# Another build-time order for the steps of a fused attention and feed-forward kernel

## The chip, the cores and the metric

The kernel runs on one core of a Trainium2 chip. The metric is the device time of one execution in microseconds (us); of several runs the median counts. TensorE (PE) multiplies matrices, with PEld for its weight loads; VectorE (DVE), ScalarE (ACT) and GpSimd (POOL) do elementwise work; SyncE (SP) issues nearly all DMAs. Each engine works through its own queue in order, and an instruction that waits holds up all that stand behind it on that engine.

## The reference

Tokens of width D = 448, S = 2048 of them, in 4 segments of L = 512; 16 heads of 28. The result is x + s * g, where s is a memory-augmented attention and g a gated feed-forward network, both of the normalized input.

```
xn = layernorm(x)
q, k, v = xn @ wq, xn @ wk, xn @ wv            # per head and segment
for each segment:                              # 16 heads
    a_dot = softmax(q k^T * scale + mask) v    # causal within the segment
    a_mem = phi(q) M / (phi(q) z + 1e-6)       # M, z: memory of earlier segments
    o     = sigmoid(beta) * a_mem + (1 - sigmoid(beta)) * a_dot
    M, z += phi(k)^T v, sum(phi(k))            # phi(t) = t + 1 if t > 0 else exp(t)
s = o @ wo
g = silu(gelu(xn @ w_gate) * (xn @ w_up) @ w_down)
out = x + s * g
```

## The kernel before

All work is first written down as steps (`Op`). A step has a name, the engines it may run on with an occupied time and a latency, the steps it depends on (`deps`), steps that must only have begun before it (`after`), buffers that it acquires, and an urgency `prio` (smaller goes first). The function `arrange` then plays the engines' queues forward with these times and picks, engine by engine, the most urgent step among those that can start within 0.2 us of the earliest. The order in which it picks is the order in which the instructions are issued; on the chip the order is fixed and only the waits are real. The times in `arrange` decide nothing but this order.

The stages on TensorE follow each other as G0, A0, A1, G1, A2, G2, A3, G3, D3 (`ORDER`). G*s* is the gate and up projection of segment *s* (`gate_up`), in 14 columns of blocks; A*s* is its attention. Into A*s* other matmuls are mixed: the projections of the next segment, the w_down matmuls of an earlier one and the output projection. To spread them over the ten groups of scores, each such step gets one group in its `after`: the share of the work that is more urgent than the step, times ten, rounded down.

Names of steps, with *s* the segment:

- `bn`, `ag`, `ep`, `pw`, `xn`, `du`, `tr`, `ev`: layernorm of a block of 128 tokens, and its transpose into `xnT` (by TensorE for segment 0, else by a DMA).
- `wq`*sg*, `wk`*sg*, `v`*sb*: projections of q, k, v on TensorE; `evwq`, `evwk`, `evv`: their evictions from PSUM. `pad`: the copy of wq and wk into padded tiles.
- `sc`*sk*: group *k* of scores on TensorE; `ex`*sk0*, `ex`*sk1*: its two exponentials on ScalarE; `mk`: the causal masks on GpSimd; `pv`*sk*: the product with v on TensorE.
- `exwq`, `exwk`, `miwq`, `miwk`, `phwq`, `phwk`: phi of q and k on ScalarE, GpSimd and VectorE; `tk`: the DMA transpose of phi(k) into `pk`; `up`, `macc`, `um`, `ma`, `mc`: the update of the memory.
- `rd`*sg* with two digits: the matmul that reads the memory; `ou`: eviction of an attention or memory result into `oa` or `om`, followed by the store of its denominators to DRAM (`den`).
- Denominators are inverted for all heads at once: `dc` loads them into the tile `dc`, `dg` and `rc` add, scale and invert on VectorE, `rd` with three digits stores the result to `rdr`, `rb` loads it broadcast into the tile `rb`. The last digit of `dc`, `dg` and `rc` is 0 for attention and 1 for memory. Then `sm` multiplies the memory part on GpSimd, `ca` the attention part on VectorE, and `cb` joins them into `oT` on GpSimd.
- `gh`, `gu`: matmuls of gate and up; `ge`: gelu on ScalarE; `hm`: the product into `hT` on VectorE, which frees the PSUM banks for a later `gu`. `dn`*sbk*: five or four w_down matmuls of token block *b*; `th`, `sg`: silu by a tanh; `wo`: output projection; `fm`, `fa`, `st`: product, sum with x, and store.
- `guard`: `sq` (ScalarE) and `rq` (VectorE) sum the squares of wq and wk, `nrm` and `nrm2` reduce them to one flag `oki`. Every engine loads the flag (`load_ok`), and the program branches on it to a slow general version, which does not run here.

The DMA steps are issued by SP in the order that `arrange` gives. Large loads at the start: x, wq, wk, wv, w_gate and w_up first; then, after the transposes of segment 1, x of segments 2 and 3, wo and two halves of w_down (`wd_in0`, `wd_in1`), all of which the w_down matmuls wait for.

Of the kernel before, what the change touches and what calls it, by code (L numbers as in the profile page):

```python
# [14 lines left out]
DRAM = bass.MemoryType.DRAM  # L15
ORDER = mybir.DependencyInfo(mybir.DependencyClass.NoSync, mybir.DependencyReason.DATA)

# [58 lines left out]
        return self.pool.aps[self.slots[i]]  # L76


SEM, SWITCH, TABLE, AHEAD = 0.06, 0.1, 1.29, 0.2
WIDE = ()  # L80
ORDER = {"G0": 0, "A0": 1, "A1": 2, "G1": 3, "A2": 4, "G2": 5, "A3": 6, "G3": 7, "D3": 8}


def arrange(ops):


    free = {e: 0.0 for o in ops for e in o.eng}
    mode, table = "full", "exp"
    blocked, left = {}, {}
    for o in ops:  # L90
        left[o] = len(o.deps) + len(o.after)
        for d in o.deps + o.after:
            blocked.setdefault(d, []).append(o)
    ready = {o: 0.0 for o in ops if not left[o]}
    done, port, lanes, pipe = [], {"DVE": 0.0, "POOL": 0.0}, [], 0.0
    while ready:
        found = []
        for o, t in ready.items():
            picks, taken = [], set()
            for b in o.acq:  # L100
                got = b.pick(taken)
                if got is None:
                    break
                t = max(t, got[0] + SEM)
                taken |= {(got[1], i) for i in got[2]}
                picks.append((b, got[1], got[2]))
            else:
                if o.kb is not None and len(lanes) >= 8:
                    t = max(t, lanes[-8] + SEM)
                for e in o.eng:  # L110
                    u = max(t, free[e])
                    if e == "POOL" or e == "DVE" and o.alone:
                        u = max(u, port["DVE" if e == "POOL" else "POOL"])
                    found.append((u, o.prio, e, o, picks))
        if not found:
            raise RuntimeError("no work can start: " + ", ".join(o.name for o in list(ready)[:20]))
        t0, _, e0, _, _ = min(found, key=lambda c: c[:2])
        s, _, e, o, picks = min((c for c in found if c[2] == e0 and c[0] <= t0 + AHEAD),
                                key=lambda c: c[1])
        occ, lat = o.eng[e]  # L120
        if e == "PE" and o.mode and o.mode != mode:
            s, mode = s + SWITCH, o.mode
        if e == "ACT" and o.act and o.act != table:
            s, table = s + TABLE, o.act
        if e == "POOL" or e == "DVE" and o.alone:
            port[e] = s + occ
        if o.kb is not None:
            pipe = max(s + lat, pipe) + o.kb / o.rate
            lanes.append(pipe)
            lat = pipe - s  # L130
        o.start, o.on, o.done = s, e, s + lat
        free[e] = s + occ
        for b, pool, slots in picks:
            b.take(slots)
        done.append(o)
        del ready[o]
        for n in blocked.get(o, ()):
            left[n] -= 1
            if not left[n]:
                ready[n] = max([0.0] + [d.done + (SEM if d.on not in n.eng else 0.0) for d in n.deps]  # L140
                               + [d.start for d in n.after])
    if len(done) < len(ops):
        raise RuntimeError("work that never gets ready")
    return sorted(done, key=lambda o: o.start)


def fast_path(tc, A_x, A_wq, A_wk, A_wv, A_wo, A_beta, B_w_gate, B_w_up, B_w_down, out):
    nc = tc.nc
    x2 = A_x.flatten_outer_dims()
# [17 lines left out]
    with ExitStack() as ctx:  # L167
# [16 lines left out]
        nhalf = const.tile([P, NB], F32, name="nhalf")  # L184
        warm = const.tile([P, L], BF16, name="warm")
        ones = const.tile([P, 1], F32, name="ones")
# [10 lines left out]
        macc = const.tile([P, G, P], F32, name="macc")  # L197
# [40 lines left out]
        nrm = const.tile([1, 2, H], F32, name="nrm")  # L238
# [4 lines left out]
        ops = []  # L243

        def op(*a, **kw):
            o = Op(*a, **kw)
            ops.append(o)
            return o
# [23 lines left out]
            return op(name, {"POOL": (t, t + 0.05)}, fn, **kw)  # L272

        def dma(name, kb, fn, **kw):
            return op(name, {"SP": (0.55, 2.0)}, fn, kb=kb, **kw)

        def turned(name, fn, **kw):
            return op(name, {"SP": (1.3, 1.5)}, fn, kb=220, **kw)
# [1 line left out]
        def at(phase, n):  # L280
            return 1000.0 * phase + n

        def A(s):
            return ORDER[f"A{s}"]

        def Gp(s):
            return ORDER[f"G{s}"]

# [39 lines left out]
        def fill(eng, name, t, pr, ap, value):  # L328
            return op(name, {eng: (t, t + 0.06)}, lambda: (
                nc.vector if eng == "DVE" else nc.gpsimd).memset(ap, value), prio=pr)  # L330
# [10 lines left out]
        for i, t in enumerate(va_t):  # L341
            va_c.append([fill("POOL", f"va{i}", 0.26, -390 + 300 * i, t[:, :, :, Dh:HP], 0.0)])
            o = va_c[i][0]
# [4 lines left out]
        o = fill("POOL", "bd", 0.4, -80, bdmask[:], 0.0)  # L348
        for i in range(HG):
            o = op(f"bd{i}", {"POOL": (0.15, 0.2)}, lambda i=i: nc.gpsimd.memset(  # L350
                bdmask[i * HP:i * HP + Dh, i * HP:(i + 1) * HP], 1.0), after=[o], prio=-79)
# [41 lines left out]
        def gates():  # L393
# [6 lines left out]
            deps=[g_op], prio=5)  # L400
# [281 lines left out]
        att = {}  # L682

        def attention(s, ph):
            steps = steps_of(0, 1) + steps_of(2, 3)
            sc, exps = [], []
            pts = {}
            acc = {g: Buf(B_, FEW if s in WIDE else ONE) for g in range(G)}
            opened, todo = {}, {g: 4 for g in range(G)}
            late, pvs = {}, []  # L690

            def scores(k):
                S2 = [Buf(B_, THREE if s in WIDE else TWO) for _ in range(2)]
                st = steps[k]
# [240 lines left out]
        def load_ok():  # L935
            got["ok"] = nc.values_load(oki[0:1, 0:1], min_val=0, max_val=1)
# [4 lines left out]
        def where_ahead(s):  # L941
            def f(nm, n):
                if s == LAST and (nm == "wv" or n > 1):
                    return at(A(s), {"wv": 1, "wq": 6, "wk": 7}[nm] + 2 * n)
                return at(A(s - 1), 20 + {"wv": 64 + 8 * n, "wq": 16 * n, "wk": 16 * n + 8}[nm])
            return f
# [5 lines left out]
        ok_op = guard(at(Gp(0), 60))  # L952
        for s in range(NSEG):
            if s < LAST:
                project(s + 1, where_ahead(s + 1), ONE)
            attention(s, A(s))
            for half in range(2):
                if s > 0:
                    phi(s, "wq", half, at(A(s), 20 + 20 * half))
                if s < LAST:  # L960
                    phi(s, "wk", half, at(A(s), 30 + 20 * half))
            if s > 0:
                read(s, at(A(s), 60))
            if s < LAST:
                update(s, at(A(s), 120))
            d = max(s - 1, 0)
            for b in range(NB):
                if s == 1 and b < 3 or s == 0 and b >= 3:
                    continue
                down(d, b, at(A(s), 12 + 24 * (b if s else 2 * b)))  # L970
            if s == 1:
                combine(0, at(A(1), 5))
            if s > 0:
                for b in range(NB):
                    finish(d, b, at(A(s), 90 + 10 * b))
            if s == 0:
                layer_norm(2, at(A(0), 100))
            else:
                gate_up(s, Gp(s))
                tabled.clear()  # L980
                combine(s, at(Gp(s), 40))
            if s == 1:
                layer_norm(3, at(Gp(s), 100))
                op("ok", {"V": (0.0, 0.0)}, load_ok, deps=[ok_op], after=[att["sc_end"]])
        for b in range(NB):
            down(LAST, b, at(8, 10 * b))
            finish(LAST, b, at(8, 10 * b + 15))
# [4 lines left out]
        for s in range(NSEG):  # L992
            work = sorted((o for o in ops if "PE" in o.eng and at(A(s), 0) <= o.prio < at(A(s), 400)),
                          key=lambda o: o.prio)
            total, sofar = sum(o.eng["PE"][0] for o in work), 0.0
            for o in work:
                k = int(sofar / total * len(att[s]))
                sofar += o.eng["PE"][0]
                if k > 0:
                    o.after.append(att[s][k - 1])  # L1000

        with tc.manual_schedule():
            for o in arrange(ops):
                if o.fn is not None:
                    o.fn()
        fast_path.ops = ops
        return got["ok"]

# [381 lines left out]
```

## Time and profile before

| | us |
|---|---|
| median of 3 runs | 249.37 (248.83 to 251.12) |
| profiled execution | 250.88 |
| its span, from the first to the last instruction | 249.0 |
| TensorE busy | 233.2 |
| VectorE, ScalarE, GpSimd busy | 161.4, 151.4, 133.5 |
| mean granted TensorE clock | 0.986 |

The times of all shown rows are microseconds from the start of the span, from one profiled execution. In a timeline row stand the start, the length, the engine, the source line, the operation with its output and inputs, and in brackets how long the engine was idle before and what ended that. The letter q behind an engine's name means its sequencer: for SP the issue of a DMA. Busy times of TensorE include the tails of matmuls that overlap the next.

### The profile page before, as it was taken

Reading aid. Unit: us, or ns where it says so; the run is one execution under the profiler, and the core shown is the slowest. Engines: PE = TensorE matmul, PEld = TensorE weight load, DVE = VectorE, ACT = ScalarE, POOL = GpSimd, SP = SyncE. Lnnn points to the kernel's source line nnn. Section 1 sums busy time; section 2 is a strip of 40 time slices with the busy share of each in tenths; the row PEclk is TensorE's granted clock in tenths of the full one; section 3 lists DMA queues with packets and bytes.
Section 4 is the critical chain, followed back from the end, with each engine's and each line's share of the span. In section 5 each row is a group of like instructions: output and inputs, shape, how many; then the busy total and the mean of one; then the engine's idle time right before and its main releaser. Section 6 shows DMA issues by size and latency. Waiting matters only on the chain.

```text
span 249.0 us, 4397 instructions
## 1 busy us (share of the span) xinstructions
PE 233.2 (94%) x1571; PEld 100.4 (40%) x1571; DVE 161.4 (65%) x289; ACT 151.4 (61%) x196; POOL 133.5 (54%) x213
## 2 busy tenths in 40 slices
PE   8899999999999979996999999999999999999990
PEld 2584433444433333442344434344334333443550
DVE  5899959958799573674734577356935564464642
ACT  2699635799889987033278787433797774333110
POOL 7304001398958989963616349931765375522640
PEclk9999999999999999999799999999999999999996
DMA  7990399620043274437300002716000002706011
GB/s 217 272 364 8 67 261 249 107 42 5 1 67 72 53 204 135 92 96 174 42 0 4 3 11 61 208 24 170 5 0 4 5 25 64 194 21 172 0 37 49
DMA packets 33429, 22.32 MB, mean 90 GB/s; under 512 B 19720, under 2 KB 29576, under 8 KB 33400
## 3 DMA queue, kind: packets, MB, share of 16 engines
q1 hardware_dynamic: 32648, 21.33, 34.7%
q10 hardware_dynamic: 752, 0.63, 0.8%
q8 instruction: 14, 0.23, 0.4%
q14 instruction: 15, 0.12, 0.2%
HBM read 15.83 MB, written 2.98 MB: 76 GB/s over the span
## 4 chain that ended last, share of the span: by engine, by line
PE 63%; DVE 8%; DMA 8%; POOL 6%; issue 6%; ACT 3%; SPq 3%; POOLq 0%; DVEq 0%; ACTq 0%
PE ps L862 13%; PE ps L492 11%; PE ps L803 7%; PE pp L803 7%; PE pp L702 5%; PE ps L764 4%; PE ps L513 4%; POOL oo L893 3%; DMA rb<-rdr 3%; PE ps L371 3%; DMA dc<-den 2%; ACT pt L718 2%; PE ps L883 2%; DVE hT L832 2%; POOL pt L729 2%
## 5 line engine op out<-in xcount | busy, mean ns | idle before, releaser
L718 ACT ACTIVATE pt<-pp 128x1024 bf16<-128x1024 f32 x80 | 77.5, 1023 | 14.8 <-PE pp L702 13.7
L729 POOL TENSOR_SCALAR_AFFINE_SELECT pt<-pt 128x256 bf16<-128x256 bf16 x128 | 56.2, 461 | 35.0 <-ACT pt L718 33.3
L828 ACT ACTIVATE gl<-pp 128x512 bf16<-128x512 f32 x29 | 16.8, 597 | 44.2 <-PE pp L818 29.6
L862 PE MATMUL ps<-wd_sb,hT 128*128 128x448 bf16 x196 | 41.6, 353 | 0.6 <-DVE om L600 0.4
L673 POOL TENSOR_TENSOR oT<-oa,om 128x512 bf16<-128x512 f32 x12 | 16.0, 1340 | 27.3 <-DVE oa L670 26.6
L862 PEld LDWEIGHTS <-hT 128*128 128x128 bf16 x224 | 20.6, 98 | 23.1 <-issue 5.2
L832 DVE TENSOR_TENSOR hT<-gl,pp 128x512 bf16<-128x512 bf16 x29 | 19.2, 679 | 13.3 <-ACT gl L828 13.3
L803 PE MATMUL pp<-xnT,wg_sb 128*128 128x512 bf16 x87 | 24.2, 388 | 2.5 <-DVE hT L832 2.1
L803 PEld LDWEIGHTS <-wg_sb 128*128 128x128 bf16 x168 | 14.8, 98 | 25.8 <-issue 11.3
L803 PEld LDWEIGHTS <-wu_sb 128*128 128x128 bf16 x168 | 16.6, 99 | 20.5 <-issue 1.2
L803 PE MATMUL pp<-xnT,wu_sb 128*128 128x512 bf16 x87 | 24.2, 388 | 0.0
L828 ACT ACTIVATE gl<-ps 128x512 bf16<-128x512 f32 x27 | 15.9, 596 | 11.4 <-DVE hT L832 4.8
L803 PE MATMUL ps<-xnT,wg_sb 128*128 128x512 bf16 x81 | 22.0, 380 | 0.0
L803 PE MATMUL ps<-xnT,wu_sb 128*128 128x512 bf16 x81 | 21.9, 379 | 0.0
L539 POOL TENSOR_SCALAR e<-e 128x1024 bf16<-128x1024 bf16 x12 | 12.5, 1039 | 14.5 <-ACT e L535 14.5
L832 DVE TENSOR_TENSOR hT<-gl,ps 128x512 bf16<-128x512 bf16 x27 | 18.2, 682 | 3.0 <-PE ps L803 1.6
L600 DVE COPY oa<-ps 128x512 f32<-128x512 f32 x16 | 11.0, 689 | 13.8 <-PE ps L764 10.0
L702 PE MATMUL pp<-qT,kT 32*128 32x512 bf16 (+3 forms) x256 | 18.6, 300 | 0.9 <-ACT pt L718 0.8
L893 POOL TENSOR_TENSOR oo<-sg,x_sb 128x448 bf16<-128x448 f32 x15 | 15.3, 1036 | 5.9 <-DVE sg L888 3.9
L626 POOL TENSOR_TENSOR om<-om,rb 128x512 f32<-128x512 f32 x12 | 14.9, 1266 | 6.1 <-DMA rb<-rdr 6.0
L492 PE MATMUL ps<-xnT,wq_pad 128*128 128x512 bf16 (+1 forms) x80 | 16.7, 337 | 0.4 <-DVE om L600 0.4
L869 DVE SCALAR_TENSOR_TENSOR sg<-th,ps 128x448 f32<-128x448 f32 x14 | 8.6, 616 | 12.2 <-ACT th L866 7.7
(94 smaller groups left out, 331.9 us busy)
## 6 DMA issues: line engine op xcount, KB each, us to landing
rb<-rdr SPq DMA_DIRECT2D x28, 256.0 KB
out_dram<-oo SPq DMA_DIRECT2D x15, 112.0 KB
wd_sb<-in_B_w_down_dram SPq DMA_DIRECT2D x2, 784.0 KB
x_sb<-in_A_x_dram SPq DMA_DIRECT2D x3, 448.0 KB
rdr<-dc SPq DMA_DIRECT2D x28, 32.0 KB
wg_sb<-in_B_w_gate_dram SPq DMA_DIRECT2D x2, 384.0 KB
wu_sb<-in_B_w_up_dram SPq DMA_DIRECT2D x2, 384.0 KB
wg_sb<-in_B_w_gate_dram SPq DMA_DIRECT2D x1, 576.0 KB
```

The source lines that it names most:

```text
L492: nc.tensor.matmul(out=bank.ap()[:, lo:hi], lhsT=wpad[nm][:, c, g * HG:(g + 1) * HG, :].rearrange("p h d -> p (h d)"), rhs=xT.ap()[:, c, l ...
L539: o = gps(f"mi{nm}{s}{half}", 1.0, lambda: nc.gpsimd.tensor_scalar(out=e.ap(), in0=e.ap(), scalar1=1.0, scalar2=0.0, op0=ALU.min, op1=ALU. ...
L626: oU[s, g, 1] = t, gps(f"sm{s}{g}", 1.22, lambda t=t, r=r: nc.gpsimd.tensor_tensor(out=t.ap(), in0=t.ap(), in1=r.ap(), op=ALU.mult), deps= ...
L673: oT[s][1].append(gps(f"cb{s}{g}", 1.22, lambda g=g, t=t, tm=tm: nc.gpsimd.tensor_tensor(out=dst.ap()[:, g, :], in0=t.ap(), in1=tm.ap(), o ...
L702: nc.tensor.matmul(out=S2[i // 2].ap(i % 2)[:, c0:c0 + n], lhsT=kT[s][0].ap()[r, g, kb * P:(kb + 1) * P], rhs=qT[s][0].ap()[r, g, kb * P:L ...
L718: nc.scalar.activation(out=dst, in_=src, func=ACT.Exp, scale=scale)
L729: nc.gpsimd.affine_select(out=v, in_=v, pattern=[[0, 2], [1, P]], compare_op=ALU.is_ge, fill=0.0, base=0, channel_multiplier=-1)
L803: nc.tensor.matmul(out=bf[fc].ap(i), lhsT=w[:, c, fc * P:(fc + 1) * P], rhs=xT.ap()[:, c, :], start=begins and c == 0, stop=not begins and ...
L828: a = act(f"ge{s}{fc}", L, lambda: nc.scalar.activation(out=gl.ap(), in_=bf[fc].ap(0), func=ACT.Gelu_apprx_tanh), func="gelu", deps=[o], a ...
L832: nc.vector.tensor_tensor(out=hT[s][0].ap()[:, fc, :], in0=gl.ap(), in1=bf[fc].ap(1), op=ALU.mult), deps=[a],
L862: nc.tensor.matmul(out=bank.ap()[:, 0:D], lhsT=hT[s][0].ap()[:, fc, b * P:(b + 1) * P], rhs=wd_sb[:, fc, :], start=(fc == 0), stop=(fc == ...
L893: o = gps(f"fa{s}{b}", 1.0, lambda: nc.gpsimd.tensor_tensor(out=oo.ap(), in0=t.ap(), in1=xs[s][:, b, :], op=ALU.add), **kw)
```

## The change

- A table `PRIO` gives 834 steps by name an urgency of their own, in place of the one that the code worked out.
- A table `STEP` gives 76 of the mixed-in TensorE steps the number of score groups that must have begun before them, in place of the computed share.
- A DMA step is counted with 0.62 us on SP and 2.1 us of latency (2.6 from 200 KB) instead of 0.55 and 2.0, and 0.5 us (`LATE`) is added before its transfer begins.
- The flag of the guard is loaded after all other steps, no longer in the middle of A1.

Operations, their shapes and their number stay as they are; the number of PSUM banks and buffers too.

```
-SEM, SWITCH, TABLE, AHEAD = 0.06, 0.1, 1.29, 0.2
+SEM, SWITCH, TABLE, AHEAD, LATE = 0.06, 0.1, 1.29, 0.2, 0.5
+PRIO = {
+    "ag00": -900.01, "ag01": -900.0, "ag02": -900.01, "ag03": -896.98, "ag10": 20.01,
...
+STEP = {
+    "dn010": 0, "dn0110": 4, "dn015": 1, "dn020": 1, "dn0210": 8, "dn025": 6, "dn030": 0,
...
-            pipe = max(s + lat, pipe) + o.kb / o.rate
+            pipe = max(s + lat + LATE, pipe) + o.kb / o.rate
...
-            return op(name, {"SP": (0.55, 2.0)}, fn, kb=kb, **kw)
+            return op(name, {"SP": (0.62, 2.1 if kb < 200 else 2.6)}, fn, kb=kb, **kw)
...
-                op("ok", {"V": (0.0, 0.0)}, load_ok, deps=[ok_op], after=[att["sc_end"]])
...
-                k = int(sofar / total * len(att[s]))
+                k = STEP.get(o.name, int(sofar / total * len(att[s])))
                 sofar += o.eng["PE"][0]
+                o.gate = len(o.after), att[s], k
                 if k > 0:
                     o.after.append(att[s][k - 1])
+        for o in ops:
+            o.prio = PRIO.get(o.name, o.prio)
...
             for o in arrange(ops):
                 if o.fn is not None:
                     o.fn()
+            load_ok()
```

Three places show how instructions move. Lines of the new file are numbered higher by 180 behind the tables.

VectorE in A1, where the memory's denominators of segment 1 are taken up (`dc_149`: `dg11`, then `rc11`; `vaug` rows are the evictions of v, `oa_112` to `oa_115` those of attention results). Before:

```order
L555 SCALAR_TENSOR_TENSOR e_103<-kT_101,e_103 128x1024
L637 TENSOR_SCALAR dc_149<-dc_149,igate 128x64
L641 RECIPROCAL dc_149<-dc_149 128x64
L518 CAST vaug_87<-ps_93 128x16x28
L869 SCALAR_TENSOR_TENSOR sg_135<-th_131,ps_91 128x448
L547 SCALAR_TENSOR_TENSOR pqT_106<-qT_99,e_105 128x1024
L518 CAST vaug_87<-ps_93 128x16x28 x2
L600 COPY oa_112<-ps_94 128x512
```

Now:

```order
L698 CAST vaug_87<-ps_92 128x16x28 x2
L1049 SCALAR_TENSOR_TENSOR sg_135<-th_131,ps_94 128x448
L698 CAST vaug_87<-ps_92 128x16x28
L780 COPY oa_112<-ps_91 128x512
L769 TENSOR_TENSOR um<-ps_92,bdmask 128x512
L780 COPY oa_114<-ps_94 128x512
L682 CAST qT_100<-ps_91 128x512
L817 TENSOR_SCALAR dc_149<-dc_149,igate 128x64
L682 CAST qT_100<-ps_92 128x512
L821 RECIPROCAL dc_149<-dc_149 128x64
```

The two steps on `dc_149` moved behind the evictions of v; a projection of segment 3 (`qT_100`) stands ahead of them.

VectorE in G1, where the first attention part of segment 1 is multiplied (`oa_112` with `rb_122`: `ca10`; `hT` rows are `hm`). Before:

```order
L832 TENSOR_TENSOR hT<-gl_128,ps_93 128x512
L555 SCALAR_TENSOR_TENSOR e_104<-kT_101,e_104 128x1024
L670 TENSOR_TENSOR oa_112<-oa_112,rb_122 128x512
L832 TENSOR_TENSOR hT<-gl_129,pp_90 128x512
L832 TENSOR_TENSOR hT<-gl_127,ps_94 128x512
L832 TENSOR_TENSOR hT<-gl_128,pp_89 128x512
L670 TENSOR_TENSOR oa_113<-oa_113,rb_123 128x512
```

Now:

```order
L1012 TENSOR_TENSOR hT<-gl_127,pp_89 128x512
L1012 TENSOR_TENSOR hT<-gl_128,pp_90 128x512
L1012 TENSOR_TENSOR hT<-gl_129,ps_93 128x512
L1012 TENSOR_TENSOR hT<-gl_127,ps_94 128x512
L1068 TENSOR_TENSOR sg_132<-sg_132,ps_92 128x448
L850 TENSOR_TENSOR oa_112<-oa_112,rb_122 128x512
L1012 TENSOR_TENSOR hT<-gl_128,pp_89 128x512
```

`ca10` moved back by four `hm` and one `fm` (`sg_132`).

The DMA queue at the start of G3, where the denominators of segment 3 are fetched (`rb` from `rdr_167` for the memory, `dc_148` for attention: `dc30`). Before:

```order
L603 DMA den_158<-oa_115 4x512
L898 DMA out_dram<-oo_138 128x448
L648 DMA rb_122<-rdr_167 128x1x512
L648 DMA rb_123<-rdr_167 128x1x512
L648 DMA rb_124<-rdr_167 128x1x512
L648 DMA rb_125<-rdr_167 128x1x512
L898 DMA out_dram<-oo_139 128x448
L634 DMA dc_148<-den_158 128x64
```

Now:

```order
L783 DMA den_158<-oa_114 4x512
L823 DMA rdr_167<-dc_149 16x8x64
L1078 DMA out_dram<-oo_139 128x448
L814 DMA dc_148<-den_158 128x64
L828 DMA rb_122<-rdr_167 128x1x512
L828 DMA rb_125<-rdr_167 128x1x512
L828 DMA rb_123<-rdr_167 128x1x512
L828 DMA rb_120<-rdr_167 128x1x512
```

The load `dc_148` moved from behind the four `rb` to ahead of them.

More of the change, by code (lines that the diff above doesn't have):

```diff
@@ L76, in ap @@
         return self.pool.aps[self.slots[i]]
-SEM, SWITCH, TABLE, AHEAD = 0.06, 0.1, 1.29, 0.2
+SEM, SWITCH, TABLE, AHEAD, LATE = 0.06, 0.1, 1.29, 0.2, 0.5
 WIDE = ()
+PRIO = {
[164 rows of a table added]
+}
+STEP = {
[10 rows of a table added]
+}
 ORDER = {"G0": 0, "A0": 1, "A1": 2, "G1": 3, "A2": 4, "G2": 5, "A3": 6, "G3": 7, "D3": 8}
```

172 rows, old and new, of tables (PRIO, STEP) are left out of this document.

## The prediction

> **What bounds the kernel now.** The page first: which engine is busy nearly always.
>
> ```profile
> PE 233.2 (94%) x1571; PEld 100.4 (40%) x1571; DVE 161.4 (65%) x289; ACT 151.4 (61%) x196; POOL 133.5 (54%) x213
> ```
>
> TensorE is busy for 233.2 of 249.0 us, so an order can win only what TensorE loses by waiting. The view by windows, cut where TensorE changes stage, shows where that is. Its columns are length, then busy time of PE, PEld, DVE, ACT and POOL (instructions in brackets), granted clock, DMA share, GB/s.
>
> ```profile
> 19.30:42.20 22.90, 22.70 (x116) 8.89 (x117) 19.94 (x48) 13.53 (x21) 4.11 (x4) 1.00 0.59 152
> 42.20:96.10 53.90, 51.15 (x437) 21.04 (x436) 42.59 (x71) 48.08 (x54) 41.41 (x73) 1.00 0.37 67
> 96.10:125.60 29.50, 27.41 (x138) 10.88 (x136) 17.75 (x26) 9.88 (x16) 20.41 (x20) 0.94 0.47 112
> ...
> 155.30:177.40 22.10, 21.99 (x116) 8.79 (x116) 12.88 (x20) 9.22 (x15) 11.92 (x12) 1.00 0.43 115
> 177.40:205.50 28.10, 26.83 (x219) 10.96 (x219) 15.60 (x25) 23.04 (x27) 16.94 (x34) 1.00 0.03 8
> 205.50:228.70 23.20, 22.67 (x121) 9.05 (x121) 10.87 (x18) 8.98 (x15) 8.60 (x11) 1.00 0.43 114
> ```
>
> The rows are G0, A0 with A1, G1, G2, A3 and G3. G0 to G3 do the same matmuls but for what is mixed in, and G2 needs 22.1 us with TensorE busy throughout. G1 needs 29.5. In A0 and A1 ScalarE is busy for 48.08 of 53.9 us, so two engines are near their limit there. The waits of that window (engine, line, releaser: us in total, times, longest) say why:
>
> ```profile
> ACT pt L718 <- PE pp L702: 5.2, 7, 1.2
> ...
> DVE dc L637 <- DMA dc<-den: 2.7, 1, 2.7
> ...
> PE ps L513 <- DVE vaug L518: 1.7, 2, 1.0
> ```
>
> ScalarE waits seven times for scores, and VectorE once, for 2.7 us, for a transfer at the head of its queue.
>
> **Part 1, A0 and A1: 3.0 us, of which 1.7 are one blocked queue.** The timeline of VectorE and TensorE there (start, length, what; in brackets the idle time before):
>
> ```profile
> 87.24 0.32 DVE L637 TENSOR_SCALAR dc<-dc,igate 128x64 f32<-128x64 f32 x1 [2.70 <-DMA dc<-den]
> ```
> ```profile
> 88.68 0.92 PE L513 MATMUL ps<-wv_sb,xnT 128*128 128x448 bf16 x4 [0.96 <-DVE vaug L518]
> ...
> 90.99 0.92 PE L513 MATMUL ps<-wv_sb,xnT 128*128 128x448 bf16 x4 [0.73 <-DVE vaug L518]
> ```
>
> `dg11` waits for its DMA; behind it stand the evictions of `v21` and `v22`, so `v22` and `v23` find no bank: 0.96 + 0.73 = 1.7 us on TensorE. In the new order `dg11` follows all four evictions of v and `evwq30`, and the wait is gone. What is late next is ScalarE, so the stage is summed on that engine:
>
> ```profile
> 84.04 1.08 ACT L535 ACTIVATE e<-kT 128x1024 bf16<-128x1024 bf16 x1
> 84.98 1.96 ACT L718 ACTIVATE pt<-pp 128x1024 bf16<-128x1024 f32 x2
> ...
> 94.79 1.94 ACT L718 ACTIVATE pt<-pp 128x1024 bf16<-128x1024 f32 x2 [0.50 <-PE pp L702]
> ```
>
> An exponential of `phi` or a tanh between two groups of scores hides the wait (84.04 to 84.98, no gap); with nothing between, 0.5 us are lost (94.79) even when TensorE is on time. The new order moves `exwq20` (0.94 us by the starts above) behind the last group of A1, where G1 leaves ScalarE time: 0.9. It leaves 8 of 19 joints bare, 8 x 0.5 = 4.0 us of waits against 5.2: 1.2. And it puts `wq30` and `wq32` (two projections of 0.87, 1.7 us, out of A2 and A3) on TensorE beside the last exponentials, where they cost 0.8 of shift: 0.9. Sum 3.0. The wait of 1.7 is inside this, since ScalarE was starved by it. The ends: 0.9 if only `exwq20` counts, 5.2 if all waits for scores go; 3.0 is near the middle, and I take it. `wq30` and `wq32` also leave A2 and A3 shorter; that is the 1.7 just counted, not more.
>
> **Part 2, G1: 3.8 us.**
>
> ```profile
> 116.28 0.69 DVE L670 TENSOR_TENSOR oa<-oa,rb 128x512 f32<-128x512 f32 x1 [3.52 <-DMA rb<-rdr]
> ```
> ```profile
> 99.83 3.19 PE L883 MATMUL ps<-wo_sb,oT 128*128 128x448 bf16 x16
> ...
> 117.62 0.81 PE L803 MATMUL pp<-xnT,wg_sb 128*128 128x512 bf16 x3 [2.09 <-DVE hT L832]
> ```
> ```profile
> 118.90:122.40 3.50, 3.50 (x13) 1.00 (x13) 3.03 (x4) 0.18 (x1) 2.19 (x2) 0.51 0.24 40
> ```
>
> `ca10` waits 3.52 us at the head of VectorE for `rb`; `hm16` behind it frees no bank, and TensorE stops for 2.09 us. 1.3 us after it starts again the granted clock is 0.51 for 3.5 us, which costs 3.5 x 0.49 = 1.7. Together 3.8; as a check, G1 without its 16 matmuls of `wo` (3.2 us by the row) is 26.3, which is 4.2 over G2. In the new order `ca10` stands after `hm19` and `fm00`, and `fm00` needs `wo00`, which TensorE now reaches about 20 us into G1; the old `rb` landed 20 us into G1, and the new request is not later (below). I take the whole 3.8; the ends are 0 and 4.2.
>
> [...] The row says: a gap of 2.09 us, then half the clock for one stretch. [...]
>
> **Part 3, A3: 1.0 us.**
>
> ```profile
> 181.16 0.39 PE L702 MATMUL pp<-qT,kT 32*128 32x384 bf16 x6 [0.51 <-ACT pt L718]
> ...
> 196.26 0.38 PE L615 MATMUL ps<-pqT,mbd 128*128 128x512 bf16 x1 [0.26 <-DVE oa L600]
> ...
> 205.49 0.39 PE L818 MATMUL ps<-xnT,wh_sb 64*128 64x512 bf16 x2 [0.35 <-DVE oa L600]
> ```
>
> Between the first two score groups of A3 the new order has four pieces of work instead of three, and the four `rd` matmuls no longer stand close together: 0.51 + 0.26 of these go, and with the third 1.1. Ends 0 and 1.1; I take 1.0.
>
> **Part 4, G3: 0.6 us.** From the timeline of the DMA queue, the chain, and VectorE:
>
> ```profile
> 210.78 2.51 SPq L648 DMA_DIRECT2D rb<-rdr  x4
> ```
> ```profile
> 105.50 1.88 DMA dc<-den
> ```
> ```profile
> 214.02 4.32 DMA dc<-den
> ```
> ```profile
> 227.34 0.69 DVE L670 TENSOR_TENSOR oa<-oa,rb 128x512 f32<-128x512 f32 x1 [4.25 <-DMA rb<-rdr]
> ```
>
> `dc30` is issued behind four transfers of `rb` and takes 4.32 us where it took 1.88 in G1. The new order issues it ahead of them: 2.5 + 2.4 = about 4.9 us earlier, and `ca30`, which held up `hm310` for 4.25 us, is on time. TensorE was mostly covered: G3 is 1.1 over G2, and I take 0.6 of that.
>
> **Part 5, what it costs: 1.1 us.**
>
> ```profile
> 9.01 0.85 DVE L380 COPY wq_pad<-hT 128x1344 bf16<-128x1344 bf16 x1
> ...
> 9.86 0.39 DVE L433 TENSOR_SCALAR xn<-x_sb,mv,rs 128x448 bf16<-128x448 bf16 x1
> ...
> 10.56 1.14 DVE L518 CAST vaug<-ps 128x448 bf16<-128x448 f32 x2
> ```
>
> At the start VectorE now does the padding of wq and one eviction (half of 1.14) before the last block of `xn`; `xn03` comes about 0.8 later, `tr03` with it, of which the first `wq00`, now ahead of `tr03`, hides 0.4: 0.5 us with the step. In G0 `phwk00` (half of a pair of 2.35) now stands ahead of `xn1` and `hm03`, and `hm02` after `hm05`, so banks come free later: 0.4, between 0 and 0.8 (G0 is 0.8 over G2 now). At the end the two halves of the last block are no longer interleaved on VectorE: 0.2.
>
> ```profile
> L936 PEldq TENSOR_LOAD <-oki x1: 492/492/492, 94.3 to 94.3; - x1
> ...
> L936 SPq TENSOR_LOAD <-oki x1: 729/729/729, 98.1 to 98.1; - x1
> ```
>
> The guard's result, loaded by every engine, leaves A1 (0.49 us on TensorE's queue, already in Part 1) for the end. There the DMA queue's 0.73 and 0.22 for the check lie beside the landing of the last store, which took 1.9 us or more in every chain above: nothing, at most 0.95 if they come after it. The longer DMA costs in the planner issue nothing themselves.
>
> **Sum.** 3.0 + 3.8 + 1.0 + 0.6 - 1.1 = 7.3 us. The profiled execution took 250.88 us, 249.0 of span and 1.9 around it, and the sum is made against it: 243.6. It lies 1.5 over the median of 249.37, from which the same sum gives 242.1. I forecast **243.0**.
>
> **Rivals.**
>
> *The clock stretch stays.* If it belongs to the time or the load and not to the gap, only 2.1 of Part 2 come: 243.0 + 1.7 = 244.7. For it: one case in the trace proves no cause. Against: it follows the only gap of 2 us after the start. Chance 0.12.
>
> *ScalarE keeps A0 and A1 as they are.* It is busy for 48.08 of 53.9 us; if the waits for scores come back elsewhere, Part 1 is nothing: 246.0. For it: the new order puts one projection between the second and third score groups, less than the 1.9 us of exponentials, so TensorE will wait there. Chance 0.20.
>
> *w_down comes late.* The rows:
>
> ```profile
> 25.72 5.25 SPq L468 DMA_TRANSPOSE xnT<-xn  x4
> ...
> 34.64 0.51 SPq L363 DMA_DIRECT2D wd_sb<-in_B_w_down_dram  x1
> ```
> ```profile
> 44.26 2.06 PE L862 MATMUL ps<-wd_sb,hT 128*128 128x448 bf16 x10
> ```
>
> The second half was issued at 34.64 and used at 44.26. The new queue puts two transposes of `pk` (1.3 us each, if they take what those of `xnT` took) ahead of those of `xnT`, and the second half last of all loads; with VectorE's later start I estimate 4 to 4.5 us later. The first `dn00` moves from 44.3 to about 49. If the load takes its 9.6 us whole, TensorE just makes it; if the transposes between slow it by half, 5 us are lost: 248. Chance 0.10.
>
> *Slower: the DMA queue blocks in G1.* `dc10` now stands behind the store `st01`, which needs `fa01` behind `miwq20`, `ma1` and `mc1` on GpSimd. From there the chain to `rb` is fixed:
>
> ```profile
> 103.11 2.25 DMA den<-oa
> ...
> 105.50 1.88 DMA dc<-den
> ```
> ```profile
> 112.76 3.43 DMA rb<-rdr
> ```
>
> From the issue of `dc` at 105.50 to the landing of `rb` at 116.2 are 10.7 us. By the durations I expect `st01` 8 to 9 us into G1 (before, `dc10` went 9.4 us into it), which fits. Past 10 us each further microsecond stops VectorE, then TensorE, and brings the slow clock: at 18 us it costs 8 + 1.7, and the kernel ends at about 252. Chance 0.08.
>
> The remaining 0.50 is the forecast, 241 to 245.5. The **range** of 239.8 to 248.5 adds the unknown ends: 2.2 more in Part 1 and 1 in Parts 2 and 4 below; above, the second rival with a wait or two that I have not found, and the third. A measurement of this kernel tells about 1% (2.5 us) from no change. Below 246.9 lie the forecast, the first rival and most of the second: 0.75; within 1%, the third and part of the second: 0.16; slower: 0.09.
>
> **What would show it.** `dg11` and `ca10` without a DMA wait of over 1 us; G1 at 25 to 26 us with a granted clock of 1.00; score waits of ScalarE in A0 and A1 near 4 us; `dc30` landing in about 2 us; A3 near 26. The forecast is wrong if a new transfer stands at the head of VectorE while TensorE needs a bank, if `dn00` waits for w_down, or if the two stages A0 and A1 still take 52 us with no more work in them.

## The result: 240.91 us, and the profile after

| | before | after |
|---|---|---|
| median of 4 runs, us | 249.26 (248.83 to 251.12) | 240.91 (240.63 to 241.43) |
| profiled execution and its span, us | 250.88, 249.0 | 240.63, 238.6 |
| TensorE busy, us | 233.2 (94%) | 226.2 (95%) |

The ratio is 0.965 (95% interval 0.960 to 0.970). The ratios here and below are of mean times and leave out a few slow runs, so they can differ a little from the quotient of two medians. From the page of the changed kernel, the busy times:

```profile
PE 226.2 (95%) x1552; PEld 99.7 (42%) x1571; DVE 156.3 (66%) x288; ACT 151.7 (64%) x197; POOL 132.2 (55%) x213
```

The view by windows of the changed kernel, cut as before; the rows are G0, A0 with A1, G1, A2, G2, A3 and G3:

```profile
19.60:41.60 22.00, 21.74 (x114) 8.91 (x116) 18.89 (x46) 14.18 (x23) 3.98 (x3) 1.00 0.50 123
41.60:94.30 52.70, 50.96 (x434) 21.40 (x438) 40.94 (x73) 47.61 (x53) 38.51 (x72) 1.00 0.44 86
94.30:120.30 26.00, 25.79 (x147) 10.87 (x148) 18.75 (x29) 10.35 (x16) 17.35 (x18) 1.00 0.49 122
120.30:147.00 26.70, 26.59 (x233) 11.76 (x236) 16.02 (x27) 22.85 (x27) 20.38 (x37) 1.00 0.04 13
147.00:169.40 22.40, 22.03 (x119) 8.94 (x122) 11.82 (x20) 9.65 (x16) 9.94 (x12) 1.00 0.46 119
169.40:195.40 26.00, 25.82 (x216) 10.68 (x216) 15.52 (x24) 22.58 (x27) 19.09 (x36) 1.00 0.04 14
195.40:217.80 22.40, 22.03 (x119) 9.08 (x122) 12.39 (x21) 9.91 (x16) 9.09 (x11) 1.00 0.46 119
```

G1 takes 26.0 us at a granted clock of 1.00, where it took 29.5 with a stretch at 0.51. Between the first matmuls of the stages lie these times (us); the column "moved" is TensorE work that the new order put into another stage, read from the starts of the moved steps (`wq30`, `wq32` 0.87 each, one block of v 0.87, `nrm` 0.32, `pv18` about 0.4):

| stage | before | after | moved | gained on the same work |
|---|---|---|---|---|
| start | 19.26 | 19.55 | | -0.3 |
| G0 | 22.94 | 22.01 | -0.3 | 0.6 |
| A0, A1 | 53.93 | 52.76 | +1.7 | 2.8 |
| G1 | 29.48 | 25.95 | +0.4 | 3.9 |
| A2 | 29.08 | 26.69 | -1.7 | 0.7 |
| G2 | 22.72 | 22.44 | | 0.3 |
| A3 | 28.08 | 26.03 | 0.0 | 2.1 |
| G3 | 23.20 | 22.35 | | 0.9 |
| D3 and the end | 20.3 | 20.8 | | -0.5 |

That is 10.4 us between the two profiled spans. The medians lie 8.4 apart; the third experiment shows where 1.7 of the difference is from. Some rows scatter from execution to execution: the start takes 18.84 to 19.72 us in the profiled executions below that keep the order of before up to G0, so the 0.3 of the first row can't be told from nothing, and G3 takes 22.6 to 23.2 us in those that keep the old order there.

VectorE of the changed kernel, with `dg11` in A1, `ca10` in G1, and `dg30` and `ca30` in G3:

```profile
94.56 0.40 DVE L817 TENSOR_SCALAR dc<-dc,igate 128x64 f32<-128x64 f32 x1
...
115.95 0.69 DVE L850 TENSOR_TENSOR oa<-oa,rb 128x512 f32<-128x512 f32 x1
...
204.16 0.25 DVE L817 TENSOR_SCALAR dc<-dc,igate 128x64 f32<-128x64 f32 x1
...
214.26 0.69 DVE L850 TENSOR_TENSOR oa<-oa,rb 128x512 f32<-128x512 f32 x1 [0.29 <-DMA rb<-rdr]
```

No bracket stands behind the first two: what they load is there when VectorE comes to them. `dg30` needs `dc30`, which therefore landed by 204.16, 8.7 us into G3; before, the chain had it land at 214.02 + 4.32, 12.9 us into G3. SyncE issued it at 200.66, so it took 3.5 us at most; that it took the 2 us of the prediction's sign is not shown. And the waits of ScalarE for scores in A0 and A1 of the changed kernel, with TensorE's for ScalarE:

```profile
ACT pt L898 <- PE pp L882: 4.0, 7, 0.8
...
PE pp L882 <- ACT pt L898: 0.9, 2, 0.6
```

### The profile page after: what moved, and what is told of

Same layout as the page of the kernel before. It is cut to its first block, busy times and chain, and to the rows that moved or that the text cites. A ratio compares the mean times of both kernels' runs of the same rounds, so it can differ in the third digit from the quotient of the medians.

```text
span 238.6 us, 4349 instructions
## 1 busy us (share of the span) xinstructions
PE 226.2 (95%) x1552; PEld 99.7 (42%) x1571; DVE 156.3 (66%) x288; ACT 151.7 (64%) x197; POOL 132.2 (55%) x213
## 5 line engine op out<-in xcount | busy, mean ns | idle before, releaser
L909 POOL TENSOR_SCALAR_AFFINE_SELECT pt<-pt 128x256 bf16<-128x256 bf16 x128 | 55.0, 450 | 25.9 <-ACT pt L898 24.2
L1008 ACT ACTIVATE gl<-pp 128x512 bf16<-128x512 f32 x29 | 16.6, 596 | 34.7 <-PE pp L998 29.7
L853 POOL TENSOR_TENSOR oT<-oa,om 128x512 bf16<-128x512 f32 x12 | 15.4, 1291 | 18.3 <-DVE oa L850 17.4
L983 PEld LDWEIGHTS <-wg_sb 128*128 128x128 bf16 x168 | 14.9, 98 | 22.4 <-issue 7.2
L983 PE MATMUL pp<-xnT,wg_sb 128*128 128x512 bf16 x83 | 22.9, 380 | 0.5 <-issue 0.5
L983 PE MATMUL pp<-xnT,wu_sb 128*128 128x512 bf16 x86 | 23.3, 379 | 0.1
L983 PE MATMUL ps<-xnT,wg_sb 128*128 128x512 bf16 x78 | 21.3, 380 | 0.5 <-issue 0.5
L1073 POOL TENSOR_TENSOR oo<-sg,x_sb 128x448 bf16<-128x448 f32 x15 | 16.4, 1100 | 6.5 <-DVE sg L1068 6.5
L882 PE MATMUL pp<-qT,kT 32*128 32x512 bf16 (+3 forms) x256 | 17.5, 300 | 1.0 <-ACT pt L898 0.9
L672 PE MATMUL ps<-xnT,wk_pad 128*128 128x512 bf16 (+1 forms) x75 | 16.1, 334 | 0.3
```

Source lines behind the costliest of these rows:

```text
L672: nc.tensor.matmul(out=bank.ap()[:, lo:hi], lhsT=wpad[nm][:, c, g * HG:(g + 1) * HG, :].rearrange("p h d -> p (h d)"), rhs=xT.ap()[:, c, l ...
L853: oT[s][1].append(gps(f"cb{s}{g}", 1.22, lambda g=g, t=t, tm=tm: nc.gpsimd.tensor_tensor(out=dst.ap()[:, g, :], in0=t.ap(), in1=tm.ap(), o ...
L882: nc.tensor.matmul(out=S2[i // 2].ap(i % 2)[:, c0:c0 + n], lhsT=kT[s][0].ap()[r, g, kb * P:(kb + 1) * P], rhs=qT[s][0].ap()[r, g, kb * P:L ...
L909: nc.gpsimd.affine_select(out=v, in_=v, pattern=[[0, 2], [1, P]], compare_op=ALU.is_ge, fill=0.0, base=0, channel_multiplier=-1)
L983: nc.tensor.matmul(out=bf[fc].ap(i), lhsT=w[:, c, fc * P:(fc + 1) * P], rhs=xT.ap()[:, c, :], start=begins and c == 0, stop=not begins and ...
L1008: a = act(f"ge{s}{fc}", L, lambda: nc.scalar.activation(out=gl.ap(), in_=bf[fc].ap(0), func=ACT.Gelu_apprx_tanh), func="gelu", deps=[o], a ...
```

## The experiments

The kernel before was run again beside each set of experiments, with medians of 248.52 to 248.85 us where it had 249.26 above. The changed kernel was not, so a difference from its median of 240.91 carries some 0.5 us of doubt.

**One part at a time, from the kernel before.** Four kernels with the order of before and single steps moved; all other rows of all engines stay.

On VectorE, in G1 (`cb10` and `cb11`, which need `ca10` and `ca11`, move with them on GpSimd):

```
-ca10 hm16 hm17 hm18 ca11 hm19 ca12 ca13
+hm16 hm17 hm18 hm19 ca10 ca11 ca12 ca13
```

> The kernel before, with one edit: in G1 the products ca10 and ca11 stand behind hm19 on VectorE, not ahead of hm16 and hm19. If the blocked queue made the gap of 2.09 us and the gap made the stretch at half clock, both go: G1 takes 29.5 - 3.8 = 25.7 us at a granted clock of 1.00, and the kernel 249.3 - 3.8 = 245.5. If the slow stretch belongs to the time or the load, only the gap goes: G1 27.4 with a stretch near 0.5 in it, the kernel 247.2. If TensorE then waits for another bank instead, G1 stays near 29 and the kernel near 249.

Measured: 247.08 us against 248.85, ratio 0.990 (0.987 to 0.993). Windows of this kernel, G1 and A2:

```profile
96.58:122.32 25.74, 25.30 (x135) 10.69 (x137) 17.92 (x25) 9.31 (x15) 19.08 (x19) 1.00 0.53 128
122.32:151.99 29.67, 28.83 (x238) 12.55 (x239) 17.19 (x28) 23.50 (x27) 16.78 (x35) 1.00 0.04 11
```

G1 takes the 25.7 us expected, at full clock, but the kernel gains 1.8 and not 3.8: A2 gives back 0.6, and most runs of before, by their times, never had the slow stretch (third experiment).

On VectorE and SyncE, in A1:

```
-dg11 rc11 evv21 sg03 phwq21 evv22 evv23      (SyncE: rd110 to rd113 behind rc11)
+evv21 sg03 phwq21 evv22 evv23 dg11 rc11
```

> The kernel before, with one edit: in A1 dg11 and rc11 stand behind the evictions of v21 to v23 on VectorE, and their four stores behind them. If the blocked queue costs its two gaps of 0.96 and 0.73 us at the end, the kernel takes 249.3 - 1.7 = 247.6. If ScalarE alone bounds the stage, TensorE's gaps move elsewhere and the kernel stays at 249.3, with A0 and A1 still near 53.9 us.

Measured: 251.89 against 248.85, ratio 1.009 (1.006 to 1.013): **slower**, which neither theory said. TensorE of this kernel at the end of A1, then TensorE and VectorE in G1, the stretch behind it, and SyncE's stores of `rd11`:

```profile
89.68 0.39 PE L702 MATMUL pp<-qT,kT 32*128 32x256 bf16 x6 [0.63 <-ACT pt L718]
...
92.07 0.39 PE L702 MATMUL pp<-qT,kT 32*128 32x512 bf16 x2 [0.48 <-ACT pt L718]
...
95.43 0.86 PE L764 MATMUL ps<-pt,vaug 128*32 128x512 bf16 x8 [0.68 <-POOL pt L729]
```
```profile
111.52 0.81 PE L803 MATMUL pp<-xnT,wg_sb 128*128 128x512 bf16 x3 [2.13 <-DVE hT L832]
...
120.37 0.81 PE L803 MATMUL pp<-xnT,wg_sb 128*128 128x512 bf16 x3 [0.81 <-DVE hT L832]
...
110.08 0.25 DVE L637 TENSOR_SCALAR dc<-dc,igate 128x64 f32<-128x64 f32 x1 [6.14 <-DMA dc<-den]
...
112.80:116.40 3.60, 3.60 (x13) 1.08 (x13) 2.33 (x2) 0.13 (x1) 2.73 (x3) 0.55 0.22 59
...
93.02 2.48 SPq L643 DMA_DIRECT2D rdr<-dc  x4
```

The same steps in the kernel before:

```profile
107.41 0.25 DVE L637 TENSOR_SCALAR dc<-dc,igate 128x64 f32<-128x64 f32 x1 [3.58 <-DMA dc<-den]
...
89.79 3.11 SPq L643 DMA_DIRECT2D rdr<-dc  x4
```

The gaps of 0.96 and 0.73 ahead of `v22` and `v23` are gone, and three others stand in their place: 0.63 and 0.48 for ScalarE and 0.68 for a mask of GpSimd, 1.79 together. A0 and A1 take 53.8 us as before. The loss comes afterwards: `rc11` is later, so SyncE issues the stores `rd110` to `rd113` from 93.0 on and not from 89.8, all that stands behind them in that queue is late, and `dg10` waits 6.14 us at the head of VectorE and not 3.58. Behind `dg10` TensorE now stops for 2.13 us, where the wait of 3.58 cost it nothing, and behind `ca10`, later in G1, for another 0.81. Before, it stopped once, for 2.09 us behind `ca10`. Both profiled executions have one slow stretch, and G1 takes 30.5 us here and took 29.5. The rest of the 3.0 us between the medians would be the slow stretch, if it came more often here: 7 of the 10 runs took 251.6 to 252.5 us and 3 took 250.1 to 250.3. Only one execution was profiled, so that is not shown.

On SyncE, in G3:

```
-rb301 rb311 rb321 rb331 st23 dc30
+dc30 rb301 rb311 rb321 rb331 st23
```

> The kernel before, with one edit: in G3 SyncE issues dc30 ahead of the four loads rb301 to rb331. If the four loads of 256 KB hold it up, it lands in about 2 us instead of 4.3, ca30 no longer waits 4.25 us for rb, and TensorE gains 0.6 us: 248.7. If TensorE was covered, the wait on VectorE goes and the kernel stays at 249.3. If the engines of the DMA are shared whatever the order, dc30 still needs 4 us.

Measured: 248.54 against 248.85, ratio 0.998 (0.995 to 1.001): no difference that can be told. `ca30` waits 1.97 us for `rb` and not 4.25, and G3 takes 22.6 us by the starts of its matmuls, 0.3 less than in the two kernels above (22.96 and 22.98). But it also takes 22.6 us in the ninth experiment, where `dc30` stands behind the `rb` as before, so this is no gain that can be put down to the move.

```profile
223.69 0.69 DVE L670 TENSOR_TENSOR oa<-oa,rb 128x512 f32<-128x512 f32 x1 [1.97 <-DMA rb<-rdr]
```

More is in the row of TensorE in G1 of this kernel, where nothing was moved, and in the windows of G1 and of the 3.9 us behind the stop:

```profile
117.89 0.81 PE L803 MATMUL pp<-xnT,wg_sb 128*128 128x512 bf16 x3 [1.98 <-DVE hT L832]
```
```profile
96.50:124.24 27.74, 25.39 (x136) 10.62 (x138) 17.36 (x26) 9.86 (x16) 20.07 (x20) 1.00 0.47 119
118.50:122.40 3.90, 3.85 (x21) 1.50 (x21) 3.90 (x6) 1.11 (x3) 2.08 (x3) 1.00 0.44 74
```

The same stop, and **no slow stretch** behind it: G1 takes 27.7 us, not 29.5. The ninth experiment, with the same order in G1, has a stop of 1.94 us there and no slow stretch either. So the 1.7 us belong to the one profiled execution of before. 29 runs of the kernel before that were made beside these four fit that: 23 took 247.9 to 249.7 us and 6 took 250.4 to 251.4; the profiled one took 250.88.

All three moves together:

> The kernel before with the three edits together (ca10 and ca11 late, dg11 and rc11 late, dc30 first). If the three queues are separate losses, they add up: 3.8 + 1.7 + 0.6 = 6.1 us, 243.2, and what is left to the changed kernel's 240.9 (2.3 us) is the new order of scores and mixed-in work. If the new order of scores is what counts and the queues matter little, this kernel stays above 246.

Measured: 249.62 against 248.85, ratio 1.001 (0.997 to 1.005). The parts do not add up. G1 has no stop now (27.15 us with a slow stretch in it), but at the end of A1 TensorE waits for GpSimd's masks, and the stretch follows that:

```profile
95.42 0.86 PE L764 MATMUL ps<-pt,vaug 128*32 128x512 bf16 x8 [1.33 <-POOL pt L729]
...
96.20:100.20 4.00, 3.67 (x20) 1.10 (x20) 0.69 (x1) 1.33 (x2) 3.43 (x6) 0.57 0.38 125
```

**Parts of the change taken back, from the changed kernel.** VectorE, in G1:

```
-hm17 hm18 hm19 fm00 ca10
+ca10 hm17 hm18 hm19 fm00
```

> The changed kernel, with one edit: in G1 ca10 stands ahead of hm17 again, where the load rb100 has not landed. If a blocked VectorE costs what the prediction says, hm17 waits until 116.2 us, TensorE reaches the block whose bank hm17 frees (gu111) at 115.2 and stops until 116.9: 1.6 us, so 242.5; with a stretch at half clock behind it 244.2. If TensorE has enough banks, nothing: 240.9.

Measured: 242.46 (ratio to before 0.976, 0.974 to 0.978), 1.55 more than the changed kernel by the medians; G1 takes 27.3 us and not 26.0. VectorE and TensorE of this kernel:

```profile
115.52 0.69 DVE L850 TENSOR_TENSOR oa<-oa,rb 128x512 f32<-128x512 f32 x1 [3.91 <-DMA rb<-rdr]
...
116.86 0.81 PE L983 MATMUL pp<-xnT,wg_sb 128*128 128x512 bf16 x3 [1.22 <-DVE hT L1012]
```

The place of one instruction costs about what was worked out (1.6), with the clock at 1.00 throughout.

TensorE and VectorE, in A1 to A3 (`evwq30` and `evwq32` go with them):

```
-pv17 wq30 wq32 gh10 ...     sc21 rd22 ...          sc31 rd30
+pv17 gh10 ...               sc21 wq30 rd22 ...     sc31 wq32 rd30
```

> The changed kernel, with one edit: the projections wq30 and wq32 leave the end of A1 and stand in A2 and A3, behind the second group of scores. If TensorE fills 0.9 us of waits with them in A1, as the prediction says, A0 and A1 get 0.8 us shorter, A2 and A3 together 1.7 longer, and the kernel takes 240.9 + 0.9 = 241.8. If they filled nothing, 240.9; if they were free there, 242.6.

Measured: 244.43 (ratio 0.984, 0.982 to 0.987), 3.5 more than the changed kernel by the medians, 2.9 between the profiled spans. TensorE of this kernel at the end of A1 and in A3:

```profile
93.04 0.39 PE L998 MATMUL pp<-xnT,wh_sb 64*128 64x512 bf16 x2 [0.91 <-ACT pt L898]
...
94.02 0.37 PE L998 MATMUL ps<-xnT,wh_sb 64*128 64x512 bf16 x1 [0.39 <-DVE oa L780]
...
176.29 0.38 PE L795 MATMUL ps<-pqT,mbd 128*128 128x512 bf16 x1 [0.78 <-DVE qT L682]
```

Without the two projections TensorE waits 0.91 + 0.39 = 1.3 us there: they were nearly free in A1, and about 1.4 of the 2.9 us is this. The other 1.4 comes from the places chosen for them here: two more waits for banks, of 0.78 (the third row) and 0.6 us. The profiled run is the fastest of the four (243.27, the others 244.0 to 244.9), and what the others lost beyond it is open.

**Half of one order, half of the other.** Both orders can be cut at the first scores of A2.

```
 order = first part of one list + all steps of the other list that are left
```

> The changed kernel's order up to the first scores of A2, then the order of before for all that is left. If each stage's gain is its own, A2 starts 4.0 us earlier than before without a slow stretch (124.2 to 120.3), A2 and A3 lose the 1.7 us of wq30 and wq32, and the rest is as before: 248.9 - 5.7 = 243.1. If A2 and A3 were shorter only since the stages ahead left VectorE and GpSimd less behind, this kernel is as fast as the changed one: near 241.

> The order of before up to the first scores of A2, then the changed kernel's for all that is left, so that wq30 and wq32 stand ahead of the first scores of A2. If each stage's gain is its own, A2 starts 1.7 us later than before (124.2 + 1.7 = 126.0) and the rest takes the 118.3 us of the changed kernel: 246.2. If A2 and A3 were shorter only since the stages ahead left VectorE and GpSimd less behind, the gain is lost: near 249.

Measured: 248.59 (ratio 0.998, 0.995 to 1.001) and 247.28 (0.995, 0.993 to 0.997). Windows of the first, A0 with A1, G1, A2 and A3:

```profile
41.88:94.84 52.96, 51.37 (x439) 21.44 (x440) 41.20 (x74) 47.67 (x53) 38.68 (x72) 1.00 0.44 87
94.84:120.80 25.96, 25.96 (x146) 10.85 (x146) 18.72 (x29) 10.33 (x16) 17.33 (x18) 1.00 0.48 122
120.80:150.89 30.09, 28.35 (x237) 12.22 (x237) 17.99 (x28) 22.96 (x27) 19.43 (x36) 1.00 0.05 11
173.72:201.56 27.84, 25.89 (x212) 10.55 (x211) 14.84 (x23) 23.15 (x27) 17.01 (x33) 1.00 0.02 4
```

and of the second, A0 with A1, A2 and A3:

```profile
42.74:99.43 56.69, 52.21 (x437) 21.18 (x437) 43.69 (x72) 48.15 (x54) 42.16 (x73) 0.97 0.35 67
...
127.37:154.13 26.76, 26.76 (x235) 11.83 (x234) 15.39 (x25) 22.84 (x26) 16.03 (x33) 1.00 0.04 13
...
176.57:202.60 26.03, 25.90 (x218) 10.69 (x218) 15.52 (x24) 22.61 (x27) 19.17 (x36) 1.00 0.04 14
```

Wherever the new list is used, its stages take the times of the changed kernel within 0.3 us, behind either first half: the gain of A2 and A3 is their own. The totals lie above what was worked out for that (243.1 and 246.2), because the halves in the old list ran worse than in the kernel before: A0 and A1 56.69 us (1.7 of it lost to a low clock, behind a stop of 1.49 us), A2 30.09 with less work in it. These halves got other PSUM banks and buffers than the kernel before gives them. That this is the cause is likely and not shown; one such loss is seen at the end of the first kernel, where the last sums, in the old order, stand behind a store that still reads their buffer.

```profile
240.83 0.69 DVE L1076 TENSOR_TENSOR oo<-sg,x_sb 128x224 bf16<-128x224 f32 x2 [1.33 <-DMA out_dram<-oo]
```

**The other parts of the diff.** The flag alone:

```
-op("ok", ..., load_ok, ...)
+load_ok() behind the loop over arrange(ops)
```

> The kernel before, with the guard's flag loaded behind all other work and nothing else moved. If TensorE's 0.49 us in A1 lies on the path and the load at the end beside the last stores, 0.5 us less: 248.4. If TensorE waits there for the masks anyway, nothing: 248.9. If the loads at the end come after the stores, up to 0.9 more: 249.8.

Measured: 247.98 against 248.71, ratio 0.996 (0.993 to 0.999): about 0.7 us by the medians. But the stage that the flag left did not get shorter: A0 and A1 take 53.94 us in the profiled execution and took 53.93, and at the end of A1 TensorE now waits for a mask of GpSimd.

```profile
94.93 0.86 PE L764 MATMUL ps<-pt,vaug 128*32 128x512 bf16 x8 [0.40 <-POOL pt L729]
```

That is the second theory, by which moving the flag gains nothing there; where the 0.7 us come from stays open. G1 of this kernel took 27.7 us, again without a slow stretch.

The tables without the costs (the edit shown, from the changed kernel), and the costs without the tables (the reverse, from the kernel before):

```
-LATE = 0.5     {"SP": (0.62, 2.1 if kb < 200 else 2.6)}
+LATE = 0.0     {"SP": (0.55, 2.0)}
```

> The changed kernel with the planner's old DMA costs (0.55 and 2.0 us, no 0.5 us ahead of a transfer), both tables as they are. If the urgencies by themselves make the order, it stays within 1 us of 240.9. If the tables fit only the times that they were made with, steps with close starts change places, instructions stand at the heads of queues before their transfers have landed, and 2 to 6 us come back: 243 to 247.

> The kernel before with the new DMA costs alone (0.62 us on SyncE, 2.1 or 2.6 of latency, 0.5 ahead of a transfer), no tables, the flag loaded in A1 as before. By its order ca10 stands behind hm19, dg11 ahead of the second and third of the evictions of v, and dc30 behind three loads of rb. If the costs do what keeps waiting steps off the head of VectorE, G1's stop goes as in the first experiment and A1 stays: 248.7 - 1.8 = 246.9. If the many other places that move as well bring stops of their own, it may end anywhere within 2 us of 248.7. If the costs are what the change is worth, near 242.

Measured: the tables with the old costs 253.12 (ratio to before 1.016, 1.011 to 1.022), 12.2 more than the changed kernel; the costs alone 245.55 against 248.82 (0.987, 0.984 to 0.991). With the old costs G0, A0 with A1, and G1 take 3.4 to 3.9 us more each than in the changed kernel. TensorE's waits for VectorE in the whole span, and VectorE and TensorE in G1, where this order has `ca10` ahead of `hm17` and `hm16`:

```profile
PE pp L983 <- DVE hT L1012: 5.1, 3, 2.0
...
122.59 0.69 DVE L850 TENSOR_TENSOR oa<-oa,rb 128x512 f32<-128x512 f32 x1 [4.54 <-DMA rb<-rdr]
...
123.94 0.38 PE L983 MATMUL pp<-xnT,wg_sb 128*128 128x512 bf16 x1 [1.73 <-DVE hT L1012]
```

and of the costs alone, VectorE in G1 and the windows of A0 with A1, G1 and A3:

```profile
119.02 0.69 DVE L670 TENSOR_TENSOR oa<-oa,rb 128x512 f32<-128x512 f32 x1 [3.37 <-DMA rb<-rdr]
119.63 1.28 DVE L832 TENSOR_TENSOR hT<-gl,pp 128x512 bf16<-128x512 bf16 x2
...
42.60:95.45 52.85, 51.15 (x438) 20.94 (x438) 42.12 (x71) 47.70 (x54) 41.39 (x73) 1.00 0.42 69
95.45:121.05 25.60, 25.60 (x139) 10.64 (x138) 14.64 (x23) 9.98 (x16) 16.34 (x17) 1.00 0.51 128
...
172.84:200.50 27.66, 26.75 (x217) 10.85 (x216) 16.42 (x26) 22.60 (x27) 19.98 (x35) 1.00 0.02 4
```

`ca10` waits 3.37 us for its load here and 4.54 there. Behind `hm19` that costs TensorE nothing; ahead of `hm16` it stops TensorE for 1.73 us, a third of the 5.1. The costs decide which of the two the planner chooses, and they put `dg11` between `evv21` and `evv22`; A0 and A1 take 1.1 us less than before. With the old costs the tables are worse than no tables.

**A version that might be faster.** From the changed kernel:

```
-sc02 dn000                        fm33224 fa33224 fm33 fa33
+dn000 sc02                        fm33 fm33224 fa33 fa33224
```

> The changed kernel with two moves: dn000 ahead of sc02 in A0, where TensorE loses 0.9 us between the halves of sc02 because ScalarE has not freed the bank, and at the end fm33 ahead of fm33224 and then the two sums, so that no VectorE instruction follows the one it needs (1.59 us for the four now, 1.29 in the order of before). If A0 is bound by TensorE there, 0.9 + 0.3 less: 239.7. If ScalarE bounds A0 and A1, only the 0.3: 240.6. If w_down has not landed by 46.6 us, TensorE waits in its order and the kernel gets slower, up to 241.5.

Measured: 240.76 (ratio to before 0.967, 0.962 to 0.971): the changed kernel's time. The loss at `sc02` is gone, but others grow by as much or more (A0 with A1 takes 53.3 us in the profiled run and not 52.8). That fits ScalarE as the limit of these stages and does not show it.

## Why the prediction came out, part by part

The forecast of 243.0 was 2.1 us above the 240.9 measured. It lies in the range, and the measured time just below the 241 to 245.5 that was given for the forecast itself. The sum was made against the profiled execution, and there the gain is 10.4 us where the parts come to 7.3. That the total still came near is in part luck: Part 2 counted 1.7 us that most runs never lose, and the time of the one profiled execution contains them too, while Parts 3 to 5 and the stages priced at nothing gave about 3 us more than was said.

- **Part 1, A0 and A1: 3.0 predicted, 2.8 found, for reasons that hold in part.** What holds: the score waits of ScalarE fell to the 4.0 us worked out, and `wq30` and `wq32` cover waits, of 1.3 us where the part said 0.9. The other half of the 2.8 was not split by an experiment. What fails is "of which 1.7 are one blocked queue": with `dg11` moved alone, ScalarE and GpSimd took all of it back. The prediction named ScalarE as the next limit but not GpSimd, whose masks stand between its products for `oT`, nor that the stores behind `dg11` move SyncE's queue into G1.
- **Part 2, G1: 3.8 predicted.** The mechanism is shown from both sides: `ca10` late takes the stop away (25.7 us), `ca10` early brings one back (1.55 us). The term was mis-sized: the stop costs 2.0 us, and the 1.7 of clock were in the profiled execution but, by their times, not in most runs. Counted against the median, the right sum was 2.0. One premise was off: the new request for `rb` goes out 17.8 us into G1 where the old one went out at 16.6, and by the fifth experiment, where the load lands 3.5 us after its issue, `ca10` escapes a wait by some 0.3 us. The place behind `hm19` is the safer part: there a wait of 3.37 us cost nothing (the costs alone). The gap does not bring the stretch each time: behind one of 1.98 us at the same place the granted clock stayed at 1.00 (third experiment).
- **Part 3, A3: 1.0 predicted, 2.1 found; and A2, priced at nothing, gave 0.7, G2 0.3.** The second half of the order run behind the old first half gives the same times, so this is the order of these stages itself. The prediction summed gaps that the timeline shows in brackets, and the step that failed is their size. A bracket counts from the modelled end of the matmul before, so it leaves part of the loss out: `sc31` starts at 180.32 and the next step at 181.49, 1.17 us for eight matmuls that take 0.33 elsewhere in A3 (`sc39`), a loss of 0.84 where the bracket said 0.51. By starts the gaps of A3 came to 2.2 us and that of A2, at `rd23`, to 0.6; nearly all are gone. The sign "A3 near 26" came true by two errors that cancel: a block of v, which the prediction did not see move from A2 to A3, fills the place of `wq32`, and the gaps gave twice what was said.
- **Part 4, G3: 0.6 predicted, 0.9 found.** The mechanism on VectorE holds, since `ca30` no longer waits 4.25 us, but what it is worth to TensorE is not shown: G3 takes 22.6 us with `dc30` moved alone and also in kernels where it stands as before, and 22.4 in the changed one.
- **Part 5: a cost of 1.1 predicted, 0.2 found.** The start cost 0.3 (0.5 said), less than it scatters by, and the end 0.5 (0.2 said), but G0 gained 0.6 where 0.4 of loss was said. Late `hm02` and early `phwk00` cost no bank, and two short waits for banks in the order of before (0.2 and 0.3 us by the starts) went. The loads of the flag do lie beside the last store, as said:

```profile
232.20 2.65 SPq L1078 DMA_DIRECT2D out_dram<-oo  x3
...
L1116 SPq TENSOR_LOAD <-oki x1: 524/524/524, 234.9 to 234.9; - x1
```

SyncE loads the flag when the last store has just been issued, and the span ends 3.2 us later. Leaving A1 gained nothing in A1 (the ninth experiment), where Part 1 counted its 0.49 us as a gain inside its sum.

- **The rivals.** The clock stretch did not stay: where the stop of G1 went and no other came, G1 ran at 1.00 (25.7 and 26.0 us). ScalarE did not hold A0 and A1 where they were. w_down was in time (the 9.6 us of the prediction run from its issue to its use, and so only bound the load from above): `dn000` starts 1.2 us earlier than estimated, behind a wait for ScalarE and none for a load.

```profile
47.51 0.39 PE L882 MATMUL pp<-qT,kT 32*128 32x256 bf16 x6 [0.63 <-ACT pt L898]
47.83 2.82 PE L1042 MATMUL ps<-wd_sb,hT 128*128 128x448 bf16 x14
```

The slower rival, SyncE's queue reaching G1, did not happen in the changed kernel, but it is what made the second experiment slow, by the chain that the rival described, from `dc10` on.

The costs were said to "issue nothing themselves". That is so, and the order they lead to was priced in the parts; but they are not a side matter, since the planner orders by them: alone they are worth 3.3 us.

## What to carry to other kernels

A wait at the head of an in-order queue cost here what stood behind it, not its own length (in the kernel before, the 3.52 us of `ca10` cost TensorE 2.09, the 3.58 of `dg10` nothing): ask which bank or buffer the next instructions free, and move the waiting one behind those. When one such wait is taken away alone, follow every queue that the moved step feeds, its DMAs above all, before counting a gain. And a list of priorities may fit only the costs that stand beside it: here the tables gave 240.9 us with the new costs and 253.1 with the old ones.

## What the runs showed of the hardware

The stretch at half clock is not a fixed price of a stop. Behind stops of TensorE of 1.33, 1.49, 2.09 and 2.13 us the granted clock fell to about 0.5 for some 3.4 us, starting 0.6 to 1.4 us after TensorE went on. Behind stops of 1.22, 1.94 and 1.98 us, the last two at the same place as the 2.09, and behind four of 1.14 to 1.95 us in the kernel with the old costs, it stayed at 1.00. So the length of the stop alone does not decide it; what does is open. At the end of the profiled executions of the kernel before and of the changed one, where TensorE stands idle for good, the clock fell 2.8 and 3.0 us after the last matmul.
